# Chunk attention and a bilinear FFN on one core: the values of the last six units computed with their axes exchanged, a column of ones beside them for the sums, and a DMA transpose into FFN layout

## The chip, the cores and the metric

The kernel runs on one core of one Trainium2 chip. The metric is the device time of one execution in microseconds (us). Before the change it is 292.78 us, the median of three runs (292.59 to 292.84). The profiled execution of the same kernel took 292.49 us, of which the profile's span holds 290.7 us.

## What is computed

Attention within chunks of 64 tokens, for 8 batches, 8 heads, 576 tokens and 64 elements per head, and then a bilinear FFN on the result (4608 tokens, width 512, inner width 1536):

```python
scores = scale * np.matmul(q_c, k_c.transpose(0, 1, 2, 4, 3))      # 64 x 64 in each chunk
attn = np.exp(scores - max); attn = attn / (sum + 1e-09)
x = np.matmul(attn, v_c)  # -> (4608, 512), heads side by side
out = (x @ w_a) * (x @ w_b) @ w_out
```

## The kernel before

**Units and blocks.** The 4608 tokens are cut into nine blocks K of 512 tokens; a block is two units u = 2K and 2K+1 of 256 tokens, and a unit is four chunks of 64 tokens with eight heads each. Attention is done unit by unit, the FFN block by block. The FFN's products use a scheme with seven in place of eight quarter products, so besides matmuls of 128x256 (line 911 for the first two weights, lines 1216 and 1054 for the third) it needs sums of weights, of x (line 871) and of the inner activations (lines 1032 and 1173), which VectorE (DVE) and GpSimd (POOL) make, and evictions of the accumulators F in PSUM, which DVE (line 949 and others) and ScalarE (ACT, line 326) make. Block 0's FFN is plain (line 822).

**One unit of attention.** q, k and v are loaded in fp32 (`load_natural`, line 355 issues it), cast to bf16 (line 326; tiles `qkb`, `vb`), and q and k are turned by a DMA transpose that SyncE (SP) issues (`turn_dma`, line 653), so that head elements lie on partitions (`qkT`). Units 0 to 3 are turned on TensorE (PE, line 501) instead. Then three groups of PE work follow, each in tiles of 64x64 that use the four quarters of the array:

- scores, 32 matmuls of 64 columns (line 685; line 673 for units 2 and 3), and ACT's exponential into `E` (line 787)
- sums, four matmuls of 512 columns with a stationary matrix of ones (line 695), whose result stands in all 64 partitions, so that it can multiply the values there; ACT makes 1/sum from it as exp(-ln(sum)) by two Ln of 512 columns (line 745) and one Exp of 1024 (line 747) into `inv`
- values, 32 matmuls of 64 columns with v stationary and E moving (line 723; line 710 for units 2 and 3). Head elements come out on partitions, which is FFN layout, and DVE multiplies them by `inv` into `xT` in two instructions of 512 columns (line 772)

**What sets the order.** Every operation is recorded with its dependencies, and a table of words written into the kernel (`ORDER_OF_ALL`) sets engine and place of each one: the letter is the engine (a PE, b ACT, c DVE, d POOL, e SP), the number is the operation, digits behind a colon are banks of PSUM. Words with f are fill matmuls on zeros (line 1529), which keep PE at work while it would wait in the first 40 us. On each engine instructions run in this order; an engine's queue never overtakes. `xT` has two buffers, for blocks of even and of odd K; SP issues all loads of this part, the transposes and the stores of results.

**Where attention stands.** From block 1 on, the attention of later blocks is strewn among the FFN's products of earlier ones: the scores, sums and values of units 12 and 13, for instance, stand among block 5's products with the first two weights and block 4's with the third.

Of the kernel before, what the change touches and what calls it, by code (L numbers as in the profile page):

```python
# [85 lines left out]
c125 e0 b1 e2 d48 b3 e4 b5 e6 d57 b51 b7 f0 f0 f0 f0 f0 f0 f0 f0 a52:0 a49:1 a58:2 b59 c60 a61:3 b62 f4 f4 f4 f4  # L86
a63:45 b64 d66 d69 b65 c53 e11 c50 e9 d75 e8 a67:6 e126 a54:70 c68 a70:2 c71 b56 a76:3 b55 b77 a105:14 c106 a98:50 b99
d78 b100 b101 d85 f6 a72:67 b73 a79:2 b80 c84 f3 f3 f3 f3 f3 f3 f3 a86:3501 b74 b90 b89 b88 c92 c87 c107 e10 d91 e145
a81:62 f7 a111:71 b112 b82 f3 f3 f3 a93:3057 c94 d132 d151 c95 a152:6 c153 b113 b114 a102:14 b83 a118:32 b97 c103 c104
b96 b119 e128 d138 a139:0 a108:75 b120 a133:6 a115:31 b134 b121 a122:24 e12 c110 c109 d13 a182:5 a164:6 c117 a170:7  # L90
e16 d17 e14 e148 b140 e18 e127 c116 a176:1 b15 c123 c124 a177:3 a183:0 b160 a178 c180 e129 a165:2 a184 c186 b135 a166
a171:4 d19 a179 a136:1 a167 c141 a142:5 b168 c181 c169 b143 b137 a172 e20 e22 b174 e24 a185 a173 a161:6 a220:32 b162
b221 b222 d21 c23 a196:5 b198 a188:1 b190 a232:76 b234 b233 b235 a200:3 c175 c25 c258 e26 c27 e146 c154 a192:4 a155:2
a193:5 a201:1 c264 c260 c262 e28 e147 d157 c187 a158:6 a189:7 c270 e30 b156 b29 c31 a204:2 a216:0 c266 c259 b202 c268
d261 b194 e32 b159 b33 a212:3 c191 e34 e150 b35 a239:46 c265 a213:7 d267 c206 c195 a197:2 a205:5 b214 c263 c272 b241
b240 a283:36 b218 a217:4 e149 e130 b163 c199 c207 e131 c144 e274 c215 d269 e36 e276 e226 f0 a236:02 c237 b285 b284
c238 d297 e40 a287:56 b286 c288 c289 a208:3 a209:7 b210 c295 c296 a299:0 d298 d37 e225 a301:2 b300 c211 a343:3 c344
a345:5 b302 c203 a348 b349 a350 b351 a352:6 a354 c219 c346 a361:7 a357 a353:3 b355 d41 b358 a363:1 d273 e38 b230 d39
c356 a369 a374:4 c359 a371 c362 a379 c370 c372 c375 d256 b364 a365 a381 b380 b366 a385 c360 c347 a383:5 e277 a376:6
a367 b382 c373 c271 c377 a407:3 a388 e42 b43 b386 e275 d280 b281 b389 a405:0 a396 b397 c387 a400 c242 c368 e44 d45 e46  # L100
a384:4 a414:6 a392:2 e224 c401 c248 b47 c250 a394:7 c254 d243 b393 e223 b229 c390 a398 a410 a423:5 b411 b395 a424 c406
c244 c255 c251 c245 d391 d249 a402 c408 c403 c399 a416 b417 b425 a435:0 a436 e282 c437 d247 a412 a438 b413 a426 b427
c418 c409 c257 a439 c440 a320:34 b321 e231 a292:10 b293 a419 b420 a430 d378 c431 a415:2 a441:3 a442 b322 a332:16 b294
b334 c421 c404 a312:40 b314 b313 a432 c252 a443 a444 a547:6 c246 a428 b445 a455 e228 e279 e278 b333 b315 b335 a456
c291 c465 c253 e227 c446 c433 d290 a316:04 a336:12 e304 c429 a458 a459 d422 c317 c318 a453:7 a451:0 b452 d434 a559:4
d475 a548 b454 c337 c338 c447 c448 a534 b535 a529:1 c473 c460 c449 a536 b537 a531:2 e305 e303 c469 c470 e325 b549 c530
a540 c541 b309 c532 a538:3 c542 a571:1 a543 c544 b457 d466 d450 d474 a550 d472 b572 e306 a539:2 e326 b551 e308 d310
c545 e324 e323 d329 a573:5 a554 c555 a552 a594 b574 a556 c557 e307 a589:0 b595 c590 b330 a591:3 c592 a596 b597 c553
a600 b601 a598:2 c602 a603 b604 a560 c561 a599:0 c605 a609:3 b610 a607:7 c608 e328 e327 d339 a611 a613 a617 c612 c618
d546 d471 d476 d533 d558 a615 c614 d319 a624:4 e311 a340:10 b341 a629 d606 d467 a562 c616 c630 e331 a500:51 b342  # L110
a492:20 b501 b494 b502 b493 c625 a635 a631 b632 c636 e484 e514 e478 a626:4 a563 a496:50 b495 e508 e482 a518:12 b520
b519 b521 e480 e477 c627 a650 e503 c468 e510 c628 c593 a638 c497 a565:4 a522:25 a566 b651 a633:1 c619 d620 e485 c498
a646:0 a634:7 e461 b564 e488 c524 c637 a567 a568 e463 b639 c523 c642 c644 c640 a648:5 a654 a652 c585 c643 c655 c645
c587 a705:2 d641 a656 e481 b569 b647 e506 a708 c657 b709 e479 e483 b490 a575 a765:1 a576 c649 a710 d489 e487 e464 c653
b711 e505 e513 c706 a714 a703:7 a712:3 a747:2 c621 c704 b715 d622 d658 c570 c577 e504 e486 d499 a717 e462 a713:7 b718
c719 a724 e664 c716 c725 a578 a745:6 a726 c727 a730 b746 b748 c766 a728 c729 b515 e509 e512 c731 a768 a579 a763:0 c764
b769 e582 a721:5 d659 c580 a770 a772:1 d586 a774 b775 a773:3 c771 e663 e507 c776 a777 a781:7 a785 a783:0 b778 c779
c782 d588 d516 d767 a789 c790 a798:4 d707 d660 a791 c792 c799 c732 a803 b786 b784 c720 c793 a805 e511 d525 b804 a787
c788 a809 b806 b810 d661 e491 a526:61 b528 a800:3 c801 c623 b527 a824 e517 a722 b723 a680:41 b681 a672:26 b674 e667
e685 e665 e584 a733:3 a734 a736 a737 c802 d780 c825 c735 b673 b682 a692:46 b675 a676:72 e686 b693 b694 e666 b695  # L120
a696:13 d669 e583 b690 a812 a807:4 c738 a741 a742 a739:6 c677 c813 c811 a826 a808:7 c678 a820:2 e684 e687 b670 c697
c698 e683 c816 c818 d817 d796 e671 c814 d815 c821 a828 a740 c827 b743 c744 c829 a749 a822:1 a750 b751 e756 d662 d819
c823 a837:3 a842 b843 b689 e691 a830 c831 c838 c832 c759 d760 a844 a839:0 c840 a848 b849 a752 a753 a846:4 c850 c754
e688 e668 d794 d835 a858 b845 a851 b859 b852 a912:5 b913 a847:7 c853 d854 a914:3 b915 a862 c863 e868 a937:0 c938 a942
c833 a860 c834 e896 e870 e867 a864 c865 a944 a939:2 c940 e897 e869 e895 d699 a946:6 b943 a948 a700:40 b949 d841 b702
a877:72 b881 b701 b882 c945 a951 b952 a959 d795 d941 d797 d679 a947:0 c950 a963 c960 c861 c964 c953 a955:7 b956
a904:45 a876:21 b878 a961 a957:6 a965 c966 d967 a972:2 b907 b908 d866 d901 b879 b909 b958 a977 c978 c962 c973 a889:4
a890 a903:50 b880 c905 d762 a926:13 c928 e758 e581 a983 a979 a974:2 c906 c929 d761 d933 a855:5 a856 c857 b980 d990
d991 a986 c975 d976 b874 a981:1 b984 b873 a982:0 a994:3 d993 e894 b900 e898 c985 c987 a883:2 a998 a884 a1002 c995 a886
a887 c999 e757 a1000 a996:7 c988 c1003 a1016 a1013:1 c1001 c997 c1014 d836 d992 d989 d954 a1004 c1005 a1018 c1019  # L130
a1011:6 d934 a1020:1 c1012 b888 b1017 a891 a892 c885 c893 a1022 b1023 e871 e899 e872 c1024 a1025 c1006 c1007 a1021:0
d1009 a1086:6 a916 a917 b910 c911 a1036 c1037 c1026 c1027 b1087 d968 a1120 b918 b1121 a1032 a1115:2 c1116 d935 b932
a919 a920 c921 b1033 a1126 e875 a927:51 b930 e902 a1051:23 b1055 b1127 c1008 c1015 c1010 b931 a1088:4 c1089 e1044
e1043 e755 e1070 e1071 d1048 d1028 a1038 c1039 d1040 e1041 d969 d1075 a1124:5 a1034 c1035 b1056 d936 e1042 a1122 b1123
c1128 a1050:21 a1078:03 b1053 b1082 b1081 d970 e1072 a1117:7 a1137 b1138 d1047 b1052 a1029:1 a1141 d971 c1118 c1142
a1077:37 b1054 c1079 a1104:06 a1129 b1130 b1083 a1133:2 a1125:5 c1131 a1030 a1135:3 b1136 c1107 e1045 b1134 c1106
c1080 e924 a1143 a1139 d1170 c1144 a1157 d1119 e1222 c1031 a1150:6 c1151 a1057:0 e1069 e923 e922 a1155 c1158 b1156
a1159:7 a1058 c1140 a1161 b1162 e1068 e925 b1074 e1249 a1152:5 c1153 a1160:6 a1164 b1165 a1060 a1176 c1059 b1177
a1189:4 d1168 a1172:5 d1169 c1163 a1180 c1166 d1167 a1178 a1191:0 a1182 e1046 d1132 d1171 c1173 a1194 c1179 e1219
a1061 b1062 c1183 c1181 b1195 d1145 a1174:2 a1063:3 a1064 b1175 c1111 c1112 c1190 a1200 a1198:6 d1184 b1201 c1192  # L140
c1202 d1193 a1065 a1066 c1067 c1085 a1196 a1199:7 e1248 c1154 d1187 d1148 a1210 b1197 a1203 b1084 a1090 a1266:4
a1264:0 b1265 c1211 a1214 c1215 a1091 e1049 b1204 a1289:5 c1205 a1294 c1295 a1212 c1290 d1146 d1206 d1147 e1073 e1221
b1110 b1092 b1267 a1216 c1217 c1213 b1226 e1247 e1076 a1093 a1094 c1095 c1253 a1296 b1297 a1229:61 b1234 a1105:57
# [30 lines left out]
def kernel(  # L174
# [32 lines left out]
    VNS = 15.5  # L207
# [7 lines left out]
    STORES = {}  # L215
    ORDER = "P0 P1 P2 P3 V0 V1 X0 q2 k2 X1 v2 X2 k3 q3 v3 O0 O1 O2 O3 O4 O5"
    JP = (0,4,7)
    INVERSES = 2
    QT = 2
    JOINT = 4  # L220
    JOINT_SPARE = 1
# [59 lines left out]
    def NI(u):  # L281

        return 0 if u % INVERSES == 0 else 2
# [1299 lines left out]
```

## Time and profile before

| | |
|---|---|
| median of three runs | 292.78 us |
| profiled execution | 292.49 us |
| its span in the profile | 290.7 us |
| PE busy | 285.5 us (98%) |
| DVE busy | 246.2 us (85%) |
| POOL busy | 185.9 us (64%) |
| ACT busy | 176.2 us (61%) |

The page of the profile gives busy time per engine and, in 40 slices, its share in tenths. The chain of work that ended last is followed back from the last instruction; its list in order of time gives start, length and name of each piece, where a piece reaches until the next one takes over, so that waiting and switching are contained in the pieces. In groups of instructions "busy" is the time in which at least one of the group ran and "mean" the duration of one; neighbours overlap in the pipeline, so that a mean can be longer than the distance from one start to the next.

### The profile page before, as it was taken

To read this page: it belongs to the slowest core of one execution; us is meant where nothing else is said; L and a number is where in the kernel's file an instruction comes from. 1 tells how busy PE (TensorE), PEld (TensorE's weight loads), DVE (VectorE), ACT (ScalarE), POOL (GpSimd) and SP (SyncE) were. 2 spreads that over 40 slices of the span, in tenths; PEclk is the share of its full clock that TensorE was granted. 3 is DMA by queue.
4 is the path that set the end of the run, shared out by engine and by line. 5 is a ranking of instruction groups with operands and counts; after the bars stand their busy time and mean duration, and the time that the engine had idled before them with its cause. 6 is when DMAs were issued, how large, how long until landed. Compare 5 with 4: busy or idle time off the path is not lost.

```text
span 290.7 us, 8704 instructions
## 1 busy us (share of the span) xinstructions
PE 285.5 (98%) x3549; PEld 233.4 (80%) x3549; DVE 246.2 (85%) x433; ACT 176.2 (61%) x307; POOL 185.9 (64%) x180
## 2 busy tenths in 40 slices
PE   7999999999999999999999999999999999999995
PEld 3455458887887888788888878888888888888884
DVE  2778899998999998998988988779988889688583
ACT  3887977966667654866683496558827642332521
POOL 4641338465498298539899879967743685787530
PEclk9999999999999999999999999999999999999999
DMA  7999999899767899976999997997950120012034
GB/s 252 390 398 402 288 297 317 195 244 236 177 132 176 226 242 208 271 167 153 211 244 191 251 220 211 205 243 166 160 116 2 40 106 2 0 68 79 3 145 145
DMA packets 137176, 55.09 MB, mean 189 GB/s; under 512 B 122160, under 2 KB 128432, under 8 KB 137136
## 3 DMA queue, kind: packets, MB, share of 16 engines
q1 hardware_dynamic: 135904, 53.43, 71.9%
q10 hardware_dynamic: 1232, 1.11, 1.1%
q8 instruction: 27, 0.44, 0.6%
q14 instruction: 13, 0.11, 0.1%
HBM read 37.75 MB, written 9.44 MB: 162 GB/s over the span
## 4 chain that ended last, share of the span: by engine, by line
PE 95%; DMA 3%; DVE 0%; POOL 0%; issue 0%; ACT 0%; ACTq 0%
PE F L911 51%; PE F L1216 25%; PE F L822 7%; DMA f<-in_k_dram 3%; PE F L1054 3%; PE F L685 2%; PE F L723 2%; PE F L695 2%; PE F L1529 1%; PE F L501 1%; PE F L630 0%; PE F L579 0%; PE F L673 0%; PE F L550 0%; PE F L710 0%; POOL qkb L326 0%
## 5 line engine op out<-in xcount | busy, mean ns | idle before, releaser
L326 ACT COPY part<-F 128x512 f32<-128x512 f32 x91 | 52.5, 591 | 52.0 <-PE F L911 36.2
L945 POOL TENSOR_TENSOR AB<-AB,bsb 128x512 bf16<-128x512 bf16 x46 | 52.8, 1155 | 21.0 <-DVE wst L1173 7.2
L949 DVE TENSOR_TENSOR bsb<-F,part 128x512 bf16<-128x512 f32 x72 | 49.1, 684 | 8.0 <-PE F L911 4.8
L1173 POOL TENSOR_TENSOR wst<-AB 128x512 bf16<-128x512 bf16 x30 | 34.3, 1155 | 13.4 <-PE F L1216 9.9
L911 PEld LDWEIGHTS <-WA 128*128 128x128 bf16 x384 | 37.1, 98 | 5.5 <-issue 1.1
L911 PEld LDWEIGHTS <-WB 128*128 128x128 bf16 x384 | 37.6, 98 | 4.6
L326 ACT COPY wst<-F 128x512 f32<-128x512 f32 (+1 forms) x40 | 22.1, 557 | 29.7 <-PE F L1216 17.9
L949 DVE TENSOR_TENSOR AB<-F,part 128x512 bf16<-128x512 f32 x48 | 32.8, 684 | 2.0 <-PE F L911 1.4
L1216 PEld LDWEIGHTS <-wst 128*128 128x128 bf16 x288 | 28.0, 98 | 3.7 <-issue 0.4
L1216 PEld LDWEIGHTS <-AB 128*128 128x128 bf16 x288 | 28.1, 98 | 3.5 <-issue 0.2
L911 PEld LDWEIGHTS <-Tb 128*128 128x128 bf16 x288 | 27.6, 98 | 3.9 <-issue 0.5
L911 PEld LDWEIGHTS <-Ta 128*128 128x128 bf16 x288 | 27.7, 98 | 3.6 <-issue 0.3
L911 PE MATMUL F<-wst,Tb 128*128 128x256 bf16 x192 | 28.9, 273 | 0.0
L911 PE MATMUL F<-wst,Ta 128*128 128x256 bf16 x192 | 28.9, 273 | 0.0
L911 PE MATMUL F<-xT,WA 128*128 128x256 bf16 x192 | 28.9, 273 | 0.0
L911 PE MATMUL F<-wst,WA 128*128 128x256 bf16 x192 | 28.8, 273 | 0.0
L911 PE MATMUL F<-wst,WB 128*128 128x256 bf16 x192 | 28.8, 273 | 0.0
L911 PE MATMUL F<-xT,WB 128*128 128x256 bf16 x192 | 28.3, 273 | 0.0
L326 POOL CAST qkb<-f 128x1024 bf16<-128x1024 f32 (+1 forms) x21 | 17.2, 835 | 15.1 <-DVE Tb L859 6.3
L1216 PE MATMUL F<-WO,AB 128*128 128x256 bf16 x192 | 24.6, 273 | 0.0
L326 DVE COPY part<-F 128x512 f32<-128x512 f32 x29 | 19.8, 686 | 2.7 <-PE F L911 2.3
L772 DVE TENSOR_TENSOR xT<-F,inv 128x512 bf16<-128x512 f32 x28 | 18.0, 684 | 2.6 <-ACT inv L747 2.1
(135 smaller groups left out, 561.2 us busy)
## 6 DMA issues: line engine op xcount, KB each, us to landing
f<-in_q_dram SPq DMA_DIRECT2D x32, 256.0 KB, 4.8
f<-in_v_dram SPq DMA_DIRECT2D x32, 256.0 KB, 4.3
f<-in_k_dram SPq DMA_DIRECT2D x28, 256.0 KB, 4.5
out_dram<-osb SPq DMA_DIRECT2D x28, 256.0 KB, 3.2
wst<-in_moe_w_b_dram SPq DMA_DIRECT2D x6, 512.0 KB, 8.4
wst<-in_moe_w_a_dram SPq DMA_DIRECT2D x6, 512.0 KB, 8.7
wst<-in_moe_w_out_dram SPq DMA_DIRECT2D x6, 512.0 KB, 6.1
out_dram<-osb SPq DMA_DIRECT2D x12, 128.0 KB, 2.4
```

The costliest lines, as they stand in the source:

```text
L326: return A.copy(out=out, in_=in_) if e == "act" else ENG[e].tensor_copy(out=out, in_=in_)
L685: T.matmul(PS[j][cl * 64:cl * 64 + 64, c:c + 64], chunk_of(u, 1, m, j, 2 * g + cl), chunk_of(u, 0, m, j, 2 * g + cl), start=True, stop=True,)
L695: T.matmul(SU[cl][j * 64:j * 64 + 64, :], ones[cl * 64:cl * 64 + 64, :], E[u % 2][cl * 64:cl * 64 + 64, j, :], start=True, stop=True,)
L723: T.matmul(PA[cl][j * 64:j * 64 + 64, c:c + 64], vb[u % 2][cl * 64:cl * 64 + 64, g * 512 + h * 64:g * 512 + h * 64 + 64], E[u % 2][cl * 64 ...
L772: op("dve", c_dve(512), lambda e, cl=cl: V.tensor_tensor(out=x.rearrange("p m (g c t) -> p c g m t", g=2, c=2)[:, cl], in0=f_of(PA[cl]).re ...
L822: T.matmul(f_of(b)[:, 0:n].rearrange("p (u t) -> p u t", u=len(us)), w[ft][:, kt, :], x[:, us[0]:us[-1] + 1, kt, :], start=(kt == 0), stop ...
L911: T.matmul(f_of(bank)[:, q * 256:q * 256 + 256], lhs(2 * g + q, kt), rhs[:, kt, :], start=(first and q == 0 and kt == 0), stop=(q == 1 and ...
L945: op(("dve", "pool"), TIMES, lambda e: ENG[e].tensor_tensor(out=dst, in0=dst, in1=b, op=MULT), r=bk, w=key, prio=-300, fast=True)
L949: op("dve", c_dve(512), lambda e: V.tensor_tensor(out=dst, in0=two(f_of(bank)), in1=two(pab[s][i]), op=ADD), r=[("ps", id(bank)), ("part", ...
L1054: T.matmul(f_of(bank)[:, 0:256], lhs[:, i, h], rhs[:, i, :], start=(first and i == 0), stop=(i == NP - 1), skip_group_check=True)
L1173: op(*long_op(hs), lambda e, i=i, x=x, y=y, o_=o_: ENG[e].tensor_tensor(out=SS[i][:, s], in0=x[:, s], in1=y[:, s], op=o_), r=fts + [(name, ...
L1216: T.matmul(f_of(bank)[:, at:at + 256], lhs[:, i, tt * 128:tt * 128 + 128], rhs[:, i, :], start=(first and at == 0 and i == 0), stop=(i == ...
```

## The change

For units 12 to 17 the sums group disappears. `vb` gets rows of 66 elements for each of 16 head columns, 64 of v and ones behind them, and the values are computed with E stationary and v with one column of ones moving: 32 matmuls of 65 columns in two halves of 16 (`part_first`, `part_second`, new line 791). Tokens now come out on partitions, and the sum of each token stands in the 65th column beside its values. DVE takes the reciprocal of four such sums at a time (line 805, 128x4) and multiplies 256 values by it (line 807), four times per unit, into `xk`, which lies in the memory of `inv`. One DMA transpose per block (`turn_x`, line 689) brings `xk` into `xT`. v of these units is loaded by `load_split` in four pieces of 64 partitions, and chunks are dealt to halves and quarters in another order (`chunk_at`).

For units 4 to 11 (`PAIRED`) q is loaded with two neighbouring tokens on one partition, in runs of 512 bytes in place of 256 (`load_paired`), and the scores matmul reads its 64 moving columns in two runs of 32. Their tokens are then in the order even, odd within a chunk, and the multiplication into `xT` (now line 863) puts them back with a step of two elements in its output. The columns of `E` are ordered by head pair first for all units from 4 on.

The table of words is a new one for the whole program; a line of it and the core of the code:

```diff
-c125 e0 b1 e2 d48 b3 e4 b5 e6 d57 b51 b7 f0 f0 f0 f0 f0 f0 f0 f0 a52:0 a49:1 a58:2 b59 c60 a61:3 b62 f4 f4 f4 f4
+c125 e0 b1 e2 b3 e4 b5 e6 e11 e9 d48 b51 b7 e8 f0 f0 f0 f0 f0 f0 f0 f0 a52:0 d57 a49:1 e126 c60 a58:2 c53 b59 a61:3
...
+    FROM = 12
+    PAIRED = range(4, FROM)
...
-    vb = [buf(f"vb_{i}", [128, 1024], BF16) for i in range(2)]
+    vb = [buf(f"vb_{i}", [128, 16, 66], BF16) for i in range(2)]
+    rec = [buf(f"rec_{i}", [128, 4, 4], FP32) for i in range(2)]
...
+    def load_paired(u, x, src):
+        t = f32[u % NF32][x].rearrange("p (h c) -> p h c", h=H)
+        (b, s0), (b1, _) = chunks[4 * u], chunks[4 * u + 1]
+        if b == b1:
+            load(t, src[b, :, s0:s0 + 256, :].rearrange("h (p r) d -> p h (r d)", r=2), f_keys(u, x), (1024, 24.0))
+            return
...
+    def turn_x(K, prio):
+        i = K % 2
+        return op("sp", 0.6, lambda e: SP.dma_start_transpose(out=xT[K % NX].rearrange("p u k (g t) -> p (u k g) t", g=2), in_=xk[i].rearrange("p u c -> p (u c)")),
...
     def chunk_of(u, x, m, j, c):
         t = qkT[u % QT][j * 64:j * 64 + 64, 8 * x:8 * x + 8, :]
+        if u in PAIRED and not x:
+            return t.rearrange("q (r m) p -> q m r p", r=2)[:, m, :, 32 * c:32 * c + 32]
...
+    def part_turned(half):
+        def part(u, prio):
...
+            def pe():
+                for m in ms:
+                    for j in range(2):
+                        for g in range(2):
+                            for cl in range(2):
+                                c, n = g, 2 * (m % 2) + j
+                                T.matmul(
+                                    f_of(PA[cl])[c * 64:c * 64 + 64, n * 65:n * 65 + 65],
+                                    E[u % 2][cl * 64:cl * 64 + 64, j, m * 128 + g * 64:m * 128 + g * 64 + 64],
+                                    vb[u % 2][cl * 64:cl * 64 + 64, g * 8 + 2 * m + j, 0:65],
+                                    start=True, stop=True,
+                                )
+            def post():
+                for cl in range(2):
...
+                    op("dve", 0.19, lambda e, got=got, i=i: V.reciprocal(out=rec[u % 2][:, i].rearrange("p (m j) -> p m j", m=2), in_=got()[:, :, :, 64]),
...
+                    op("dve", c_dve(256), lambda e, got=got, i=i, cl=cl: V.tensor_tensor(
+                        out=xk[K % 2][:, u % 2].rearrange("p (m s j d) -> p m s j d", m=4, s=2, j=2)[:, ms.start:ms.stop, cl], in0=got()[:, :, :, 0:64],
+                        in1=rec[u % 2][:, i].rearrange("p (m j) -> p m j", m=2).unsqueeze(3).to_broadcast([128, 2, 2, 64]), op=MULT),
...
-            slot(AT + u, (part_sums, u), (part_scores, u + 1), fixed=True)
+            if u < FROM:
+                slot(AT + u, (part_sums, u), (part_scores, u + 1), fixed=True)
+            else:
+                slot(AT + u, (part_scores, u + 1), fixed=True)
```

**PE, units 12 and 13.** Names are tiles with their buffer numbers; LDWEIGHTS loads the stationary operand. Before, at the sums of these two units, between a product of the FFN on `Ta` and one on `WA`; each of the four F stands twice:

```order
L911 LDWEIGHTS Ta_0_113
L911 MATMUL F4_65<-wst_7_107,Ta_0_113 128x256
L695 LDWEIGHTS ones_70
L695 MATMUL F2_63<-E_0_84,ones_70 64x512
...
L695 MATMUL F1_62<-E_0_84,ones_70 64x512
...
L695 MATMUL F0_61<-E_1_85,ones_70 64x512
...
L695 MATMUL F3_64<-E_1_85,ones_70 64x512
```

Eight matmuls of 512 columns that stood alone among the FFN's products are gone, and the table has no such group after unit 11. In the changed program the first half of unit 13's values stands right behind an FFN product and is followed, without an FFN product between, by the scores of unit 12 (16 and 32 matmuls; rows of each F once):

```order
L1307 MATMUL F5_66<-WO_101,spare_sum_110 128x256
L791 LDWEIGHTS E_1_87
L791 MATMUL F2_63<-vb_1_81,E_1_87 64x65
...
L791 MATMUL F3_64<-vb_1_81,E_1_87 64x65
...
L731 LDWEIGHTS qkT_0_82
L731 MATMUL F6_67<-qkT_0_82 64x64
...
L731 MATMUL F4_65<-qkT_0_82 64x64
```

The scores of unit 13 stand alone ahead of this, and the other 48 turned matmuls of the block in one group behind it. So a block of these units has three groups among the FFN's products, as before, but of other sizes.

**DVE, the same two units.** Before, the four multiplications into `xT` stand among evictions of the FFN's accumulators:

```order
L949 TENSOR_TENSOR bsb_93<-F5_66,part_86 128x2x256
L772 TENSOR_TENSOR xT_0_89<-F3_64,inv_87 128x2x4x64
L949 TENSOR_TENSOR AB_1_92<-F5_66,part_86 128x2x256
L772 TENSOR_TENSOR xT_0_89<-F6_67,inv_0_88 128x2x4x64
L772 TENSOR_TENSOR xT_0_89<-F0_61,inv_0_88 128x2x4x64
L772 TENSOR_TENSOR xT_0_89<-F7_68,inv_87 128x2x4x64
```

Now twelve of the sixteen new instructions stand in one row, without an eviction between, on six banks of PSUM (the twelfth, a multiplication, is not shown):

```order
L1040 TENSOR_TENSOR AB_1_92<-F7_68,part_88 128x2x256
L805 RECIPROCAL rec_1_85<-F2_63 128x4
L805 RECIPROCAL rec_1_85<-F3_64 128x4
L805 RECIPROCAL rec_0_84<-F5_66 128x4
L807 TENSOR_TENSOR inv_97<-F5_66,rec_0_84 128x2x128
L805 RECIPROCAL rec_0_84<-F6_67 128x4
L805 RECIPROCAL rec_0_84<-F4_65 128x4
L807 TENSOR_TENSOR inv_97<-F2_63,rec_1_85 128x2x128
L807 TENSOR_TENSOR inv_97<-F6_67,rec_0_84 128x2x128
L807 TENSOR_TENSOR inv_97<-F4_65,rec_0_84 128x2x128
L807 TENSOR_TENSOR inv_97<-F3_64,rec_1_85 128x2x128
L805 RECIPROCAL rec_0_84<-F7_68 128x4
```

**SP, block 8.** The transpose into `xT` for the last block stands between stores of results, in the changed program:

```order
L683 DMA_TRANSPOSE qkT_0_82<-qkb_0_78 128x16x128
L1110 DMA out_0_dram<-osb_0_94 128x512 x2
L1110 DMA out_0_dram<-osb_2_96 128x512
L689 DMA_TRANSPOSE xT_0_89<-inv_97 128x16x128
L1110 DMA out_0_dram<-osb_2_96 128x512 x2
```

There are three of these transposes, one each for blocks 6, 7 and 8. On PE the first product that reads the transposed `xT` stands 126 matmuls of 256 columns behind the last turned matmul in block 6, 116 in block 7 and 82 in block 8. Fills are 24 where there were 25: the one ahead of the values of units 2 and 3 is gone, the seven ahead of line 630 are four ahead of a transpose and three behind it.

More of the change, by code (lines that the diff above doesn't have):

```diff
@@ L91 @@
[L91 to L95, printed above, removed]
@@ L387, in load_v0 @@
                 v[K, :, g * 128:(g + 1) * 128, :].transpose([1, 0, 2]),
-                [("f32", half, 2, 2 * n + i) for i in range(2)], (1024, VNS), issue=0.55,
+                v_keys(half, 2 * n, 2 * n + 1), (1024, VNS), issue=0.55,
             )
```

291 lines of the change are left out of this document (175 added, 116 removed).

## The prediction, made before the changed kernel ran

> **What bounds the kernel now.** I read the page first: busy time, the 40 slices, the chain that ended last.
>
> ```profile
> span 290.7 us, 8704 instructions
> PE 285.5 (98%) x3549; PEld 233.4 (80%) x3549; DVE 246.2 (85%) x433; ACT 176.2 (61%) x307; POOL 185.9 (64%) x180
> PEclk9999999999999999999999999999999999999999
> PE 95%; DMA 3%; DVE 0%; POOL 0%; issue 0%; ACT 0%; ACTq 0%
> ```
>
> PE is busy for 98% of the span at full clock, and 95% of the chain is PE. Then the waits of PE, all that the view holds:
>
> ```profile
> PE F L1529 <- DVE zero L1321: 1.3, 1, 1.3
> PE F L501 <- POOL qkb L326: 0.5, 2, 0.3
> PE F L501 <- ACT qkb L326: 0.2, 1, 0.2
> ```
>
> All lie in the start, since line 1529's wait is its first fill and line 501 turns units 0 to 3. So from then on PE's own list is the time: what leaves it is gained, unless something else becomes late. Now the chain in order of time, around units 12 and 13 and at two plain stretches:
>
> ```profile
> 168.16 0.44 PE F L911 x4
> 168.60 0.67 PE F L685 x64
> 169.27 2.29 PE F L911 x20
> 171.56 0.56 PE F L695 x8
> 172.12 0.98 PE F L911 x8
> ...
> 174.19 0.67 PE F L723 x64
> 174.85 1.42 PE F L911 x12
> ...
> 183.69 3.49 PE F L911 x32
> ...
> 199.63 0.64 PE F L685 x64
> ```
>
> The plain stretch gives 3.49 / 32 = 0.109 us for one product of 256 columns. Behind a group of 64x64 tiles the same products take 2.29 for 20 (plain 2.18), 0.98 for 8 (0.87), 1.42 for 12 (1.31): 0.11 us more each time. So a group among the FFN's products costs its own time and 0.11 us for the way back. Groups of other sizes, and a place where groups touch (units 8 and 9):
>
> ```profile
> 38.52 0.34 PE F L695 x4
> ...
> 117.64 0.38 PE F L685 x32
> 118.02 0.98 PE F L911 x8
> 119.00 0.66 PE F L1216 x6
> 119.65 0.37 PE F L685 x32
> 120.24 2.73 PE F L1216 x24
> 123.31 0.65 PE F L723 x64
> 123.96 0.98 PE F L911 x8
> ```
>
> 32 matmuls alone are 0.38, 64 are 0.67. From 119.65 to 120.24 lie 32 scores and four sums: 0.59, so sums that touch another group add 0.22 and no way back.
>
> **Units 12 to 17 on PE.** Before: three blocks with three groups each, 0.67 + 0.56 + 0.67, then 0.64 + 0.56 + 0.64 (the row at 199.63; values alike), then 0.67 + 0.56 + 0.67: 5.64, and nine ways back, 0.99: 6.63 us. After: two blocks have 32 alone, 32 scores with 32 values, 32 alone: 0.38 + 0.67 + 0.38 = 1.43 each. Block 6 has 32, 48 and 48; 48 is halfway between 0.38 and 0.67, 0.525, so again 1.43. With nine ways back, 4.29 + 0.99 = 5.28 us. **Gain 1.35 us.** The 65th column: were columns all, 1/64 of the 0.29 us that 32 more matmuls add, for six units, is 0.03; I take nothing, since 9 ns per matmul is more than a quarter of the 0.109 us / 4 that 64 columns take in one quarter of the array. That E is now the stationary operand changes no count: 32 weight loads of 64x64 each, before and after.
>
> **Units 4 to 11 on PE.** The order regroups them. Units 4 and 5: scores apart, two times 0.38 + 0.11 in place of 0.67 + 0.11, a loss of 0.20. Units 8 and 9 were 0.38, 0.59 and from 122.97 to 123.96 0.99 (four sums and 64 values), with three ways back 2.29; now 0.67 + 0.56 + 0.67 + 0.33 = 2.23, a gain of 0.06. Units 6 and 7 were two groups of 32 and two of 32 with sums, 2 x 0.38 + 2 x 0.59 + 0.44 = 2.38, now 2.23: 0.15. Together **nothing (0.01 gained)**. Moving columns in two runs of 32: no row shows such a read; lower bound nothing, upper bound that these 8 x 32 matmuls go from 9 ns to, say, 12 (0.8 us). I take nothing, as the nearest rows are the contiguous ones.
>
> **The first phase (block 0's FFN, line 822).** The fill ahead of the values of units 2 and 3 goes, and one group of four sums now touches 32 scores:
>
> ```profile
> 39.66 0.38 PE L1529 MATMUL F<-zero 128*128 128x512 bf16 x1
> 39.97 0.74 PE L710 MATMUL F<-E,vb 64*64 64x64 bf16 x64
> ```
>
> From 39.66 to 39.97, 0.31 us. The sums: 0.34 + 0.11 and 0.38 + 0.11 become 0.59 + 0.11: 0.24. **Gain 0.55 us.** The fill covered a wait for `vb`, and it can come back as one, so the bounds are 0.24 and 0.55. I take the upper: the loads of weights and of v of units 2 and 3 keep their place in SP's queue within two transfers, and PE reaches these values only half a microsecond sooner.
>
> **The start.** The fills ahead of line 630:
>
> ```profile
> 10.99 1.51 PE F L1529 x7
> 12.50 0.55 PE F L630 x16
> ```
>
> They are split around a transpose now, four and three, so PE reaches line 630 at 12.5 either way, or up to 0.3 us sooner, as part of the 0.5 us that line 501 waited (above) is now filled. Two memsets of `vb` stand ahead of DVE's zeros; the first fill comes up to 0.2 us later, and the wait of 0.2 for ACT's cast hides that. I take nothing.
>
> **DVE, ACT, POOL.** What these cost at places where PE waits for nobody:
>
> ```profile
> L745 ACT ACTIVATE inv<-F 128x512 f32<-128x512 f32 x32 | 17.6, 608 | 3.2 <-PE F L695 3.2
> L747 ACT ACTIVATE inv<-inv 128x1024 f32<-128x1024 f32 x16 | 16.8, 1071 | 0.2
> L592 DVE TENSOR_TENSOR xT<-F,inv 128x256 bf16<-128x256 f32 x4 | 1.4, 416 | 0.0
> L560 DVE RECIPROCAL inv<-F 128x256 f32<-128x256 f32 x2 | 3.5, 1748 | 0.0
> L772 DVE TENSOR_TENSOR xT<-F,inv 128x512 bf16<-128x512 f32 x28 | 18.0, 684 | 2.6 <-ACT inv L747 2.1 <-PE F L723 0.3
> ```
>
> ACT loses 12 x 0.608 + 6 x 1.071 = 13.7 us. DVE: 684 against 416 ns leaves a fixed 148 ns per instruction; a reciprocal is 6.2 ns per element beyond it (1748 - 148 over 256), so one of 4 elements is 0.17 us. A unit goes from 2 x 0.684 = 1.37 to 4 x 0.416 + 4 x 0.17 = 2.35: 0.98 more, 5.9 us for six units, where a multiplication right behind its own reciprocal may wait up to another 0.1 (24 times, 2.4). DVE's room there:
>
> ```profile
> 156.00:183.00 27.00, 27.00 (x366) 23.46 (x364) 23.29 (x40) 16.82 (x28) 24.35 (x23) 1.00 1.00 218
> 183.00:210.00 27.00, 27.00 (x366) 23.37 (x364) 22.67 (x39) 18.50 (x32) 20.34 (x20) 1.00 0.99 187
> 210.00:237.00 27.00, 27.00 (x365) 23.38 (x364) 23.98 (x43) 14.23 (x26) 15.82 (x15) 1.00 0.28 80
> ```
>
> The busy figures are PE, its weight loads, DVE, ACT, POOL, then come the clock, the share of the DMA engines and GB/s. DVE is busy 23.29, 22.67 and 23.98 of 27 us: 11 us of room against 5.9 to 8.3, and the new order gives ACT, which is lighter, some of DVE's copies of accumulators (22 stay of 29 into `part`). So **nothing** on PE's path, if the bursts shown in the order are short enough. [...]
>
> Line 863 (16 instructions for units 4 to 11) writes with a step of two elements. No row has such a write; the lower bound is 0.684 as now, the upper twice that, 11 us of DVE over 100 us. I take the lower, as line 592 writes in pieces too and costs what its size says. [...]
>
> **The transposes into xT.** SP's transposes so far:
>
> ```profile
> L653 SPq DMA_TRANSPOSE qkT<-qkb x14: 1327/2107/3520, 53.6 to 210.6; - x14
> DMA to landing us min/median/max: 3.7/4.2/7.3
> ```
>
> Same size as the new ones (16 tiles of 128x128). After the last turned matmul DVE needs at most its unit's 2.35 us, the DMA 4.2: 6.5 us, at worst 9.7. PE has 126, 116 and 82 products of 0.109 us to do before it reads: 13.8, 12.7 and 8.95 us. In the median all three are in time, in the worst case block 8 is 0.7 late. I take nothing. v of units 12 to 17 in 24 loads of half the partitions costs SP 12 more issues, q of units 4 to 11 fewer packets; neither is on the chain.
>
> **The sum.** 1.35 + 0.01 + 0.55 = 1.91 us, from 292.49 of the profiled execution to 290.58. The end (last product, DVE, store) has the same steps in both. The median of the runs lies 0.29 above the profiled one, so I expect 290.87, given as 290.9, with its own range of 290.3 to 291.5. A change of under 0.2%, 0.59 us, could not be told from none.
>
> **The rivals.**
>
> *DVE's bursts hold PSUM (0.16).* The twelve instructions in a row take 6 x 0.17 + 6 x 0.416 = 3.5 us, up to 4.1 with waits, on six of eight banks, while PE goes on to products that need banks. It has about 2 free banks, 2 x 0.44 us and more where sums go to a bank in use. For: DVE is busy 84 to 89% there. Against: four multiplications of 0.684 with evictions between took as long, and PE never waited. If PE stands 0.3 to 0.4 us at each of the three blocks, 1 us is lost: 291.9. [...]
>
> *The transpose comes late: slower (0.10).* SP never overtakes: ahead of block 8's transpose stand three stores that wait for results. If these hold it by the longest issue in the trace, 3.5 us, with the slowest landing the way is 3.5 + 2.35 + 7.3 = 13.2 us: 4.2 late in block 8, 0.5 in block 7, so 290.9 + 4.7 = 295.6. It ends on the other side once the waits add up to 2.5 us (1.91 + 0.59), that is when block 8's way exceeds 11.5 us. Against it: DMA is busy only 0.28 in the stretch 210 to 237.
>
> *The new order starves PE elsewhere (0.12).* Every engine's list is new. In the first phase PE comes half a microsecond sooner to the same weights and values; the 0.55 are not gained and as much again is lost: 290.9 + 1.1 = 292.0. For it: line 501's waits show that the first phase runs close to its loads. Against it: in the old order PE never waited for a cast weight.
>
> The change does what it says on PE: the order shows no sums after unit 11, so I give no chance to the opposite.
>
> **How the numbers follow.** Forecast 0.62, the three rivals 0.16, 0.10 and 0.12. Faster by over 0.2% (below 292.19): the forecast, half of the first rival (0.08) and half of the third (0.06): 0.76. Within 0.2%: the other 0.08 and 0.03: 0.11. Slower: 0.10 and 0.03: 0.13. The range leaves out the second rival and the ends: 290.3 to 292.6.
>
> **What would show it.** Right: groups at line 791 of 0.38 alone and 0.67 with scores; PE's waits still only in the start; the products of lines 1002 and 1307 at 0.109; line 805 near 0.17, line 807 at 0.416, line 863 at 0.684; first product of block 6, 7 and 8 with no idle time before it. Wrong: PE idle ahead of line 1002 or 1307 with DVE named (first rival) or the DMA of line 689 (second); line 863 near 1.4; groups of line 731 longer than 0.67 for 64.

## The result, and the profile after

| | before | after |
|---|---|---|
| median of the runs | 292.81 us (292.59 to 293.4) | 291.12 us (290.8 to 291.47) |
| profiled execution | 292.49 us | 291.09 us |
| its span | 290.7 us | 289.3 us |

The ratio is 0.9939, with a 95% interval of 0.9921 to 0.9958: about 0.6% faster, 1.7 us by the medians and 1.4 us between the two profiled executions. The forecast was 290.9 us.

The page of the changed kernel, busy times and the chain that ended last:

```profile
PE 284.5 (98%) x3524; PEld 233.2 (81%) x3524; DVE 244.5 (85%) x465; ACT 177.0 (61%) x304; POOL 176.4 (61%) x171
PE 97%; DMA 1%; DVE 0%; ACT 0%; issue 0%
```

PE is still busy for 98%, with 25 matmuls fewer. PE's waits in the changed kernel, all that the view holds:

```profile
PE F L1636 <- DVE zero L1412: 1.3, 1, 1.3
```

The two waits of line 501 are gone from the view. It leaves out short ones, though, as the chain of the first phase shows (start, length, piece):

```profile
17.36 3.31 PE F L913 x14
20.67 0.02 issue
20.70 0.70 DVE bsb L329
21.40 0.04 issue
21.44 2.75 PE F L913 x12
...
39.66 0.81 PE F L756 x64
```

From 20.70 to 21.40 the chain runs over DVE: PE had four transposes to do there (line 527, 0.22 us elsewhere) and then stood until DVE had emptied a PSUM bank. The values of units 2 and 3 (line 756) took 0.81 us where before they were 0.67 behind a fill. The chain around units 12 and 13, and 14 and 15, in place of the sums:

```profile
169.93 0.25 PE F L791 x16
170.19 0.26 PE F L731 x32
...
198.07 0.37 PE F L731 x32
198.44 0.27 PE F L791 x30
```

16 turned values with 32 scores take 0.25 + 0.26 = 0.51, and 32 of each 0.37 + 0.27 = 0.64. 32 turned values alone, at 201.43, are 0.38. The new operations by line (min, median and max in ns, then first and last start):

```profile
L805 DVE RECIPROCAL rec<-F x24: 149/170/183, 170.2 to 232.6; 128x4 f32<-128x4 f32 x24
L807 DVE TENSOR_TENSOR inv<-F,rec x24: 391/414/425, 170.5 to 233.5; 128x256 bf16<-128x256 f32 x24
L863 DVE TENSOR_TENSOR xT<-F,inv x16: 701/720/739, 71.0 to 150.9; 128x512 bf16<-128x512 f32 x16
L689 SPq DMA_TRANSPOSE xT<-inv x3: 1566/1627/1777, 176.1 to 234.0; - x3
DMA to landing us min/median/max: 3.7/3.8/3.8
```

**Where the time went, stretch by stretch.** Start to start in the two traces: the first phase begins at 17.58 before and 17.36 after; it lasts 24.80 and 24.78 us; from there to the start of the last product it is 244.80 and 243.76; the tail is 3.53 and 3.40. The differences, 0.22 + 0.02 + 1.04 + 0.13, make the 1.4 us of the span. The first cannot be read from these two profiles: in those of the experiments below the first phase begins anywhere from 17.14 to 18.51 with the new order, and at 18.48 in the other profile with the old one. What the medians say of it comes with the first experiment. The tail lies between 3.39 and 3.65 with the new order and at 3.51 in the other profile with the old one. What the trace shows to be the change's own is the part behind 42 us, 1.04. That is 1.43 from units 12 to 17 and 0.07 from units 4 to 11, less 0.44 of new short stands of PE among its products (0.49 after, 0.05 before), the longest 0.16 at 79.73 and 0.10 at 133.02.

### The profile page after: what moved, and what is told of

Its sections match the earlier page's. It is cut to its first block, busy times and chain, and to the rows that moved or that the text cites. A ratio compares the mean times of both kernels' runs of the same rounds, so it can differ in the third digit from the quotient of the medians.

```text
span 289.3 us, 8674 instructions
## 1 busy us (share of the span) xinstructions
PE 284.5 (98%) x3524; PEld 233.2 (81%) x3524; DVE 244.5 (85%) x465; ACT 177.0 (61%) x304; POOL 176.4 (61%) x171
## 4 chain that ended last, share of the span: by engine, by line
PE 97%; DMA 1%; DVE 0%; ACT 0%; issue 0%
PE F L1002 51%; PE F L1307 26%; PE F L913 7%; PE F L1145 3%; PE F L527 2%; PE F L731 2%; PE F L1636 1%; DMA f<-in_k_dram 1%; PE F L741 1%; PE F L769 1%; PE F L791 1%; PE F L656 0%; PE F L576 0%; PE F L553 0%; PE F L605 0%; PE F L756 0%
## 5 line engine op out<-in xcount | busy, mean ns | idle before, releaser
L329 ACT COPY part<-F 128x512 f32<-128x512 f32 x98 | 55.9, 589 | 55.1 <-PE F L1002 36.0
L1036 POOL TENSOR_TENSOR AB<-AB,bsb 128x512 bf16<-128x512 bf16 x44 | 50.5, 1158 | 40.1 <-DVE AB L1040 12.8
L1264 POOL TENSOR_TENSOR wst<-AB 128x512 bf16<-128x512 bf16 x31 | 35.8, 1162 | 7.8 <-DVE AB L1036 4.1
L329 ACT COPY wst<-F 128x512 f32<-128x512 f32 (+1 forms) x42 | 23.5, 570 | 26.3 <-DVE osb L1335 8.7
L329 ACT CAST qkb<-f 128x1024 bf16<-128x1024 f32 (+1 forms) x23 | 22.3, 975 | 3.7 <-DMA f<-in_k_dram 3.7
L878 ACT ACTIVATE E<-F 128x512 bf16<-128x512 f32 x32 | 17.6, 602 | 8.6 <-PE F L731 8.4
L329 POOL CAST qkb<-f 128x512 bf16<-128x512 f32 (+1 forms) x20 | 15.8, 805 | 9.8 <-DVE WA L329 3.7
```

What stands on the lines that cost most here:

```text
L329: return A.copy(out=out, in_=in_) if e == "act" else ENG[e].tensor_copy(out=out, in_=in_)
L878: op("act", c_act(512), lambda e, j=j: A.activation(out=E[u % 2][:, j], in_=f_of(PS[j]), func=AF.Exp, scale=scale), r=[("ps", id(PS[j]))], ...
L1036: op(("dve", "pool"), TIMES, lambda e: ENG[e].tensor_tensor(out=dst, in0=dst, in1=b, op=MULT), r=bk, w=key, prio=-300, fast=True)
L1264: op(*long_op(hs), lambda e, i=i, x=x, y=y, o_=o_: ENG[e].tensor_tensor(out=SS[i][:, s], in0=x[:, s], in1=y[:, s], op=o_), r=fts + [(name, ...
```

## The experiments

Each is compared with the changed kernel's 291.12 us; their runs of the kernel before had medians of 292.88 to 293.46.

**Sums back on PE alone.**

```diff
+                for j in range(2):
+                    for cl in range(2):
+                        T.matmul(f_of(PA[cl])[j * 64:j * 64 + 64, 260:512], ones[cl * 64:cl * 64 + 64, :],
+                                 E[u % 2][cl * 64:cl * 64 + 64, j, 0:252], start=True, stop=True)
```

> The changed kernel, with sums put back on PE alone: behind each half of the turned values (units 12 to 17, twelve halves) stand four matmuls with the stationary ones and 252 columns of E, whose result nobody reads; ACT and DVE get no work from them, and the order is the same. Theory (the time is PE's own list, and these sums were the 1.4 us that units 12 to 17 gave): four sums of 512 columns that touch another group cost 0.22 us, so 252 columns cost 0.11, twelve times 1.3 us: 292.4 us, nearly the time before. Rival (the gain came from the lighter ACT, from DMA or from the new order, and PE had room): within 0.2 us of the changed kernel, 291.1.

Measured: 292.38 us (292.16 to 292.64), ratio to before 0.998 (0.9969 to 0.9991). The chain of this run, with the sums as line 799 and the names of lines shifted by eight:

```profile
198.90 0.13 PE F L791 x16
199.03 0.11 PE F L799 x4
199.14 0.13 PE F L791 x15
199.27 0.11 PE F L799 x4
```

Twelve groups of 0.107 are 1.28 us, and the time went up by 1.26, though ACT's lighter load, the DMA and the new order were left as they were. So behind the start PE's list is the time.

The same run says something of the start. Its first phase and what follows up to the last product take 24.77 + 245.04 us, 0.2 more than the 24.80 + 244.80 of the kernel before; yet its median is 0.50 us below the 292.88 of the kernel before in the same series (0.26 to 0.91 by the interval of the ratio). So, as an estimate, some 0.5 us or more were gained ahead of the first phase or outside the span, by the new order there and not by the sums. A part is outside the span, where the runs of the kernel before have 1.8 to 2.6 us in this series and those of this run 1.7 to 1.9. No run shows what made it: the waits of line 527 (0.7 and 0.5 us here, none in the changed kernel) are not it, since the first phase begins at 17.39 here and at 17.36 there.

**q of units 4 to 11 as before.** The load becomes two transfers of 256-byte runs under the same word of the table, and the four places that use the pairing (cast, scores' operand and result, multiplication) are switched off:

```diff
-            load(t, src[b, :, s0:s0 + 256, :].rearrange("h (p r) d -> p h (r d)", r=2), f_keys(u, x), (1024, 24.0))
+            op("sp", 0.5, lambda e: [piece(2 * g, 128, b, s0 + 128 * g) for g in range(2)][-1], w=f_keys(u, x), land=(1024, 24.0), prio=place["at"], behind=held)
...
-                if u in PAIRED:
+                if u in TURNED:
```

> The changed kernel with its other half undone: q of units 4 to 11 loaded in 256-byte runs as before, cast straight, scores read in one run of 64 columns, the multiplication into xT without the step of two; places of all operations as in the changed kernel. Theory (this half is off PE's list and worth nothing): 291.1, within 0.2; the multiplication falls from 0.719 to 0.684 us and the scores stay at 0.64 to 0.67. Rival (fewer packets and earlier q are part of the gain): q lands later, PE waits ahead of scores, 0.3 us or more slower, 291.4 to 292.

Measured: 291.18 us (290.95 to 291.71). The multiplication, eight lines further down here, lost the cost of its step of two:

```profile
L871 DVE TENSOR_TENSOR xT<-F,inv x16: 679/680/692, 70.8 to 150.6; 128x512 bf16<-128x512 f32 x16
```

720 against 680 ns, 0.64 us of DVE in all, changes nothing, nor do the packets that are saved. This half of the change is worth nothing in this order.

**The fill of the kernel before.** One word `f0` ahead of the values of units 2 and 3 is taken out of the old table:

```diff
-e276 e226 f0 a236:02 c237
+e276 e226 a236:02 c237
```

> The kernel before, without its fill of 0.31 us ahead of the values of units 2 and 3. Theory (the fill only covered DVE's cast of v, which ends at 39.84 there): PE waits in its place, and at most 0.1 us is gained: 292.7. Rival (as predicted, the fill stood on PE's own list): 0.31 us sooner, 292.5.

Measured: 292.72 us (292.44 to 293.58), ratio to before 0.9987 (0.9973 to 1.0). A gain of 0.31 us would be 0.9989, one of 0.07 us 0.9998, so the times do not separate the two expectations; the trace does. The profile of this run begins 0.9 us later, so it is read by its own chain:

```profile
40.05 0.70 DVE vb L326
...
40.79 0.74 PE F L710 x64
```

The timeline has the idle time ahead of the weight loads of these values, and what ended it:

```profile
40.79 0.62 PEld L710 LDWEIGHTS <-vb 64*64 64x64 bf16 x64 [0.57 <-DVE vb L326]
```

Where the fill was, PE now stands until DVE has cast v. From the scores at the phase's middle to its end it is 0.07 us shorter (6.93 against 7.00), of the fill's 0.31.

**Two waits of the first phase.** One word is moved on PE, so that a product takes the bank that was free; the digits 1 and 4 then change places in the rest of the table. One word is moved on DVE:

```diff
-a178 a165:2 c180 e26 a161:4 c19 a171:1 e28 a172
+a178 a165:2 c180 e26 c19 a171:4 a161:1 e28 a172
...
-b283 a208:4 d144 c207 e274 b234 a209:3 e224 c163
+b283 a208:1 d144 c163 c207 e274 b234 a209:3 e224
```

> The changed kernel with two places of its order changed in the first phase: the turn of q or k that stands at 20.93 goes behind the next two products (it had taken the last free PSUM bank, so that these products waited for DVE to empty one), and on DVE the cast of v that ended at 39.74 goes ahead of the multiplication at 38.45. Theory (the 0.55 us that the first phase did not give went into these two waits, 0.29 and 0.15, which the order makes and no load): 0.4 us sooner, 290.7. Rival (the first phase is bound by its loads and casts, so that a wait taken away comes back further on): 291.1, with new waits ahead of line 527, 913 or 756 of the same size. Third: only the first of the two is gained, since v lands at 38.23: 290.85.

Measured: 291.32 us (291.08 to 291.49): nothing gained. The chain in the first phase of this run:

```profile
39.22 0.70 DVE AB L928
39.92 0.04 issue
39.96 0.44 PE F L756 x30
```

The wait at 20.93 shrank from 0.29 to 0.08 us, but the values stood at 39.96 for 0.38 us: DVE, which had been idle until 38.62, cast v first and came to its multiplication at 39.22, and that one empties a bank that the second unit's values need. The rival holds for this pair of edits: the time came back as another wait.

**One of them, and one at 79.73.** Only PE's word is moved, as above, and on DVE a sum goes behind a multiplication:

```diff
-c537 d465 c466 b533 a539 b306 b540 c541 c538
+c537 d465 b533 a539 b306 b540 c541 c466 c538
```

> The changed kernel with two waits taken out by order alone: the turn that stands at 20.93 goes behind the next two products (as in the earlier run, but DVE's cast of v stays where it was), and at 78.66 DVE's sum of AB goes behind the multiplication of the accumulator that PE waits for at 79.73. Theory (where a wait goes and nothing behind it is late, PE's list is the time): at 20.93 0.2 to 0.3 is gained and of it what v's landing at 38.2 to 38.6 and the two DVE operations behind it (0.69 each) allow, 0.3 at most by the time line 1002 begins; at 79.73 0.16 is gained and stays: together 0.3 to 0.45, 290.7 to 290.8. Rival (the first phase is bound by v's landing and what DVE does behind it): PE stands at line 756 as long as it came sooner, and only the 0.16 stays: 290.95.

Measured: 290.69 us (290.6 to 290.99), ratio to before 0.9913 (0.9888 to 0.9937). The chain of this run at the places of the two waits:

```profile
17.29 4.16 PE F L913 x18
21.45 0.30 PE F L527 x4
21.75 2.16 PE F L913 x10
...
39.38 0.81 PE F L756 x64
```

The DVE piece is gone from 20.70, the first phase lasts 24.57 in place of 24.78 us, and the 0.81 of line 756 stayed, no longer and no shorter, since DVE's multiplication ahead of the cast comes sooner by as much as PE does. Behind 42 us it is 243.60 in place of 243.76: the 0.16 at 79.73. So 0.37 us by the trace, and 0.43 by the medians of two series, whose ratios to before overlap in their intervals (0.9921 to 0.9958 and 0.9888 to 0.9937); the trace carries this. Of the 0.53 us that the first phase gave too little, 0.21 was the order's and could be had back.

**Each transpose into xT twice.**

```diff
-lambda e: SP.dma_start_transpose(out=xT[K % NX]..., in_=xk[i]...),
+lambda e: [SP.dma_start_transpose(out=xT[K % NX]..., in_=xk[i]...) for _ in range(2)][-1],
```

> The changed kernel with each of the three transposes into xT issued twice in a row, the second over the first. Theory (these transposes have 7.3, 4.9 and 2.6 us to spare in blocks 6, 7 and 8): the second lands about 3.8 us after the first, so that only block 8 is late, by 1.2 us: 292.3, with PE idle ahead of block 8's first product and nowhere else. Rival (SP's queue is the tight one: loads behind the transposes come late too): waits also ahead of scores or values of units 14 to 17 and 2 us or more in all, 293 or over. Third (the room is larger than the trace makes it): 291.1.

Measured: 296.38 us (295.9 to 298.99), 5.3 us more where 1.2 was expected. The rival comes nearer in time. Its waits ahead of scores and values are not there, but late loads are, in another place. First DVE's wait for the transposes in this run (us in total, times, longest):

```profile
DVE wst L962 <- DMA xT<-inv: 5.8, 3, 2.5
```

PE's own waits, the first and the one for the transpose:

```profile
PE F L1002 <- ACT part L329: 3.2, 2, 2.1
...
PE F L1002 <- DMA xT<-inv: 0.3, 1, 0.3
```

And the timeline's row at block 8:

```profile
248.22 0.43 DVE L962 TENSOR_TENSOR wst<-xT 128x512 bf16<-128x512 bf16 x1 [2.55 <-DMA xT<-inv]
```

PE hardly waits for the transpose itself. The first reader of `xT` is DVE, with a sum of x (line 962), and everything queued behind that sum, evictions of accumulators above all, waits with it. In the changed kernel these sums start here:

```profile
182.53 0.42 DVE L962 TENSOR_TENSOR wst<-xT 128x512 bf16<-128x512 bf16 x1
212.00 0.41 DVE L962 TENSOR_TENSOR wst<-xT 128x512 bf16<-128x512 bf16 x1
238.66 0.41 DVE L962 TENSOR_TENSOR wst<-xT 128x512 bf16<-128x512 bf16 x1
```

The transposes landed at 179.86, 209.49 and 237.75, so the room was 2.7, 2.5 and 0.9 us, not the 7.3, 4.9 and 2.6 that PE's first product has. The second landing, 3.7 us after the first, is late in all three blocks.

That is the smaller part of the cost. From start to start of its products PE stood 6.2 us longer in this execution than in the changed kernel, and 3.5 of them are the two waits for ACT, 1.3 and 2.2 us, the 3.2 of the view above:

```profile
217.10 1.99 ACT L329 CAST vb<-f 128x1024 bf16<-128x1024 f32 x2 [2.85 <-DMA f<-in_v_dram]
...
219.63 0.61 PE L1002 MATMUL F<-wst,Tb 128*128 128x256 bf16 x4 [1.10 <-ACT part L329]
...
222.91 1.04 ACT L329 CAST qkb<-f 128x1024 bf16<-128x1024 f32 x1 [2.35 <-DMA f<-in_k_dram]
```

ACT's copies of accumulators, for which PE waits, are queued behind its casts of v and k, and these waited for loads. SP had issued the loads of v at 213.33 and that of k at 217.36, where in the changed kernel it is 207.41 and 211.42, since the transposes began at 207.80 in place of 205.74 and, being two, held SP's queue for 5.49 us in place of 1.63; in the changed kernel the same two casts start without waiting. So the rival's mechanism, loads behind the transposes that come late, is there, and it reaches PE through ACT's queue.

**More and less on DVE.** Each of the 24 multiplications twice, each of the reciprocals twice, both twice, and reciprocals left out:

```diff
-lambda e, got=got, i=i, cl=cl: V.tensor_tensor(...),
+lambda e, got=got, i=i, cl=cl: [V.tensor_tensor(...) for _ in range(2)][-1],
...
-lambda e, got=got, i=i: V.reciprocal(out=rec[u % 2][:, i]..., in_=got()[:, :, :, 64]),
+lambda e, got=got, i=i: [V.reciprocal(out=rec[u % 2][:, i]..., in_=got()[:, :, :, 64]) for _ in range(2)][-1],
...
-lambda e, got=got, i=i: V.reciprocal(out=rec[u % 2][:, i]..., in_=got()[:, :, :, 64]),
+lambda e, got=got, i=i: V.memset(rec[u % 2][:, i], 1 / 64) if u < 14 else None,
```

> The changed kernel with each of the 24 multiplications of turned values made twice: 24 times 0.33 us (from one start to the next) to 0.416 more on DVE, 7.9 to 10 us, where DVE is idle for 11.2 us of 156 to 237. Theory (DVE has room on average, as the prediction took it): within 0.3 us of 291.1. Rival (the prediction's first: the burst of a unit's operations holds PSUM banks): PE stands behind each of the three bursts for the 2 us or so that they get longer, less two free banks of 0.44: 1 us or more each, 294 or over.

> As the last, with the 24 reciprocals made twice as well: 9.9 to 14 us more on DVE against 11.2 us of idle time. Theory (average room): up to 3 us over the changed kernel, 291.1 to 294. Rival (bursts hold banks): more than the run with multiplications alone by the reciprocals' 24 times 0.08 to 0.17 us, in full.

> The changed kernel with the 24 reciprocals made twice, the multiplications once. From the runs before: the second reciprocals cost 4.9 us beside doubled multiplications, 0.20 each, while the doubled multiplications alone cost 7.2 of the 7.9 us that they add. Theory (DVE's operations stand within 0.06 to 0.2 us of the place where PE waits for a bank, so that work added there is paid but for that): 24 times 0.08 to 0.20, less some 0.2 for each of the three blocks: 2 to 4 us more, 293 to 295. Rival (the 11.2 us of idle DVE take it, and only the 10 us of the doubled multiplications were too much): 291.1 to 291.6.

> The changed kernel with less on DVE: the 8 reciprocals of units 12 and 13 become memsets of 1/64, the 16 of units 14 to 17 are left out, so that the values of these units are divided by 64 in place of their sums. Theory (in the changed kernel PE waits nowhere for these operations, so that what they cost now is nothing): 291.1, within 0.2. Rival (DVE's added work is paid in part already): 291.1 less 0.1 to 0.2 for each of 16 reciprocals, 1.6 to 3.2 us less, 288 to 289.5.

Measured, with DVE's busy time from each page beside it:

| | time | against 291.12 | DVE busy against 244.5 |
|---|---|---|---|
| reciprocals left out (memsets in units 12 and 13) | 291.06 us | -0.06 | -1.8 |
| reciprocals twice | 293.42 us | +2.30 | +3.8 |
| multiplications twice | 298.29 us | +7.17 | +9.7 |
| both twice | 303.19 us | +12.07 | +14.0 |

PE's waits with the multiplications doubled:

```profile
PE F L1002 <- DVE bsb L1040: 1.5, 3, 0.9
PE F L1002 <- DVE inv L807: 0.9, 3, 0.5
PE F L791 <- DVE inv L807: 0.8, 2, 0.6
```

PE waits for banks that the bursts hold or that evictions behind them empty. Of 3.8 us added some 1.5 were free, and of the next 5.9, in a run with other operations added, 4.9 were paid. DVE's 11.2 us of idle time in these stretches are no room: the theory of an average room falls, and the first rival's mechanism is real, though it does not act in the changed kernel, where less work on DVE gains nothing. How close it stands shows at block 8 (rows of the changed kernel):

```profile
226.01 0.68 DVE L1040 TENSOR_TENSOR AB<-F,wst 128x512 bf16<-128x512 f32 x1
226.62 0.44 PE L791 MATMUL F<-vb,E 64*64 64x65 bf16 x32
```

The multiplication ends at 226.69. The second 16 of the 32 turned matmuls write the bank that it empties, and they start at 226.76: 0.07 us to spare. At 198.40 it is 0.08, and at 173.16, 0.20.

**Two further waits.** To the run with two waits taken out, three sums on DVE move behind two multiplications, and two copies on ACT change places; then the copies alone:

```diff
-c250 c369 c254 c248 c255 c402 a406 b407 a403:7 c404
+c250 c369 c402 a406 b407 a403:7 c404 c254 c248 c255
...
-c825 b839 d790 e577 c834 a743 a840:3 e894 c813 c788 d789 b837
+c825 b837 b839 d790 e577 c834 a743 a840:3 e894 c813 c788 d789
```

> The run with two waits taken out, and two more taken out by order alone: at 58.84 to 59.93 three sums on DVE go behind the two multiplications of accumulators that ACT's copies at 61.24 wait for (PE stood 0.06 and 0.06 at 61.88 and 62.36), and at 131.89 two copies on ACT change places (PE stood 0.10 at 133.02). Theory (PE's list is the time, and each of these waits stands by itself): 0.2 less than that run, 290.5. Rival (what is moved back makes another wait of the same size): 290.7, with new waits ahead of line 1002 or 1307.

> The run with two waits taken out and the change of places of two copies on ACT at 131.89 alone, without the three sums on DVE that the run with four waits moved. Theory (the 1.0 us that PE stood at 67.70 there came from those sums: POOL, which waits for the last of them, came late and then ran beside a sum on DVE that took 1.64 in place of 0.69 us): no wait at 67, PE's stand of 0.10 before 133 gone, 290.6. Rival (the copies on ACT or the run's later start made it): the wait at 67 comes again, 291.5.

Measured: 291.56 us (291.22 to 293.01) with all four, 290.69 us (290.37 to 290.79) with three. The four waits went, and a new one of 1.0 us came at 67.70 (rows of the run with four):

```profile
62.49 2.46 POOL L1036 TENSOR_TENSOR AB<-AB,bsb 128x512 bf16<-128x512 bf16 x2 [4.83 <-DVE wst L1264]
63.86 1.64 DVE L1249 TENSOR_TENSOR WO<-WO 128x1024 bf16<-128x1024 bf16 x1
67.70 0.60 PE L1002 MATMUL F<-wst,WA 128*128 128x256 bf16 x4 [0.95 <-DVE AB L1040]
```

POOL waits for the last of the three sums and so came late, ran into DVE's sum of weights (line 1249, 0.69 us in the run with two waits out), and DVE's evictions behind it were late. Without the three sums moved there is no wait at 67, and the 0.10 before 133 is gone. By medians three waits out is no faster than two; the kernel with two or three, 290.7 us, has the lowest median of the study, 0.4 us below the changed one.

## Why the prediction was right, and where its reasons were not

**Units 12 to 17: right.** 1.35 us were forecast and 1.43 came by the groups of the trace; putting only the sums back cost 1.26. The groups were as said: 0.38 alone, 0.64 with scores, way back 0.10. The 65th column costs nothing that shows, 0.38 for 32 as with 64 columns.

**Units 4 to 11: right.** 0.01 forecast, 0.07 by the trace, and undoing the data side changed nothing. Scores in runs of 32 took 0.64 to 0.67 us for 64, the lower bound. The write with a step of two took 0.720 us and not 0.684, at the lower bound but for 5%; without the step, in the run with q as before, it took 0.680, 40 ns less.

**The first phase: wrong.** The step "**Gain 0.55 us** ... I take the upper" failed: the phase was 0.02 us shorter, below even the lower bound of 0.24. The sums that touch scores gave 0.22 from product to product, as said but for 0.02. The fill was mis-sized: of its 0.31 only 0.216, what a product of 512 columns takes from start to start, was its own, because the last one ahead of a group of 64x64 tiles takes 0.31, fill (39.66 to 39.97 before) or product (39.28 to 39.59 after). And it stood in a wait for DVE's cast of v, of which 0.14 came back at line 756; 0.07 was left, in the old kernel without its fill as in the changed one. What took the rest is the wait for a bank at 20.93, 0.29, which the new order made: 0.22 + 0.07 - 0.29, and 0.02 among the products. That is the third rival as far as the 0.55 go. Its other half came too, as 0.44 us of short stands behind 42 us; it was put down as 0.12 likely and is what happened, in smaller size.

**The start: "I take nothing" failed, as far as the medians show.** The profiles spread too much to tell, but the run with the sums back puts some 0.5 us ahead of the first phase or outside the span. What made it stays open.

**DVE: the right number for a wrong reason.** The durations held (0.170 and 0.414 us against 0.17 and 0.416), and the cost was nothing. But "11 us of room against 5.9 to 8.3" does not carry it: 3.8 us more cost 2.3. What the rows show in its place is an order in which the banks that the turned matmuls write are emptied 0.07 to 0.2 us before PE takes them. That this is the measure of the room is argued and not shown: 1.5 us of what was added were free, more than these three places give. The rival's "about 2 free banks" was no better a measure. In the run with the reciprocals doubled, 24 more of four elements cost 2.3 us, 0.1 each.

**The transposes: the right number with the wrong reader.** They were in time, with 3.7 to 3.8 us to landing against 4.2 taken. The step "PE has 126, 116 and 82 products ... to do before it reads" was wrong, since DVE reads `xT` first, for the sums of x; the real room is 0.9 us in block 8. The second rival, slower, was therefore nearer than its price said: the doubled transposes add 3.8 us to each way and cost 5.3. It also counted the way to `xT` alone, while most of PE's added stands, 3.5 of 6.2 us in the profiled execution, came by the loads of v and k behind the transposes in SP's queue.

**The sum.** 290.9 against 291.12, a gain of 1.69 us by the medians where 1.91 was added up. The groups gave 1.43 + 0.07 against 1.36; 0.53 was missing in the first phase and 0.44 was lost in stands; some 0.5 of the start and 0.13 of the tail, both put at nothing, came instead. Two errors of about half a microsecond each on one side were covered by one on the other, and that is luck: without the start's half microsecond the sum would have come out near 291.6, above the forecast's own range.

## What to carry to other kernels

When one engine's list is the time, count what leaves that list, and check each filler or cover for what it stands in front of: of the fill's 0.31 us here only 0.07 was gained, 0.14 came back as a wait and 0.10 as a longer last product ahead of the values. Room on another engine is not its idle share (DVE was idle for 11.2 us, and 3.8 us more on it cost 2.3); as far as these runs show, look at the time between its release of a buffer and the moment at which the bound engine takes it. The first reader of a transfer may be an engine that is not the bound one, with evictions queued behind it (DVE, with 0.9 us of room in block 8 where PE had 2.6). What holds a DMA queue longer also delays the loads behind it (two transposes held SP's for 5.49 us, one for 1.63), and these can reach the bound engine through a third one's queue (3.5 us of PE's stands, by ACT). A new order brings its own short waits, which views with a threshold hide (0.29 us at 20.93 and 0.16 at 79.73 here); find them by start-to-start gaps, take them out one at a time, and see whether each stays out.

## What the hardware showed that was not expected

**The clock fell after two short stands.** In the profiled run with doubled transposes PE stood for 1.3 us until 219.63 and for 2.2 us until 224.49, with products between. From 225.6 to 229.0 each product took 0.213 us, twice 0.109 (us, busy PE, clock, DMA share, GB/s):

```profile
224.00:225.50 1.50, 1.01 (x10) 1.00 0.24 55
225.50:227.00 1.50, 1.50 (x10) 0.52 1.26 286
227.00:229.00 2.00, 2.00 (x12) 0.51 0.04 7
```

16 products lost 1.6 us by it, and that execution took 298.99 us where the median was 296.38. That was one execution of seven: the other six show a granted clock of 0.998 to 1.000 in the mean, this one 0.994. Whether PE stood as long in those six no trace shows, and what lowered the clock here is not shown either.

**A sum on DVE can take 1.64 in place of 0.69 us beside one on POOL.** In the run with four waits out it began at 63.86 inside POOL's two sums (62.49 to 64.95) and ended at 65.50, 0.55 us after them. A shorter sum on DVE at 63.53, beside the same two, took 0.42 us, as in the run with two waits out (at 61.96). What made the other one longer is not shown.
